# Three eighths of the last w2 block moved to 16 partitions on four DMA engines, and w_mod loaded in two pieces instead of three

## Chip, cores, metric

One core of one Trainium2 chip. The metric is the device time of one execution in microseconds (us). PE is the matrix engine, DVE, ACT and POOL are the vector, scalar and general engines, SP is the sync engine, which issues the loads. Every run also lists its **span**, the time from the first to the last instruction that the profiler recorded. Time minus span is called *outside*.

## The reference, cut to what matters

```python
mod = silu(c) @ w_mod                       # c: 2 x 1024, w_mod: 1024 x 6144
h = layernorm(x) * (1 + ca) + sa
x = x + ga * attention(h, k_cache, v_cache, wq, wo)   # 4 KV heads, 32768 positions, 32 query heads, batch 2
h = layernorm(x) * (1 + cb) + sb
y = gelu(layernorm(h) @ w1 + b1)            # 3584 wide
x = x + gb * (y @ w2 + b2)                  # w2: 3584 x 1024
```

Two tokens meet 178.28 MB of caches and weights, so this is a kernel that streams. `w_mod` opens the stream and `w2` closes it.

## The kernel before

The stream is issued from the sync engine (SP). The pieces that the change and the argument touch:

```python
WMOD_ITEMS = ((0, 1), (1, 4), (4, 8))       # rows of w_mod per load: lines of 12, 36, 48 KB a partition
W2_ITEMS = ((0, 8, 96), (8, 16, 112), (16, 24, 128), (24, 27, 144), (27, 28, 150))   # blocks of w2 per load
...
w2_v = B_w2.rearrange("(p j) n -> p j n", j=FT)      # 28 blocks of 128 rows x 1024 columns
for m, (j0, j1, off) in enumerate(W2_ITEMS):
    add(("w2", m), [j1 - j0, DM], w2_v[:, j0:j1, :], off * KB)
```

w2 comes in five loads: blocks 0 to 7, 8 to 15, 16 to 23, 24 to 26, and 27 alone. The tail multiplies the first 16 blocks with the activations as the stationary side, turns that result into columns with eight fp32 matmuls, and adds the last 12 blocks with the weights as the stationary side:

```python
for g in range(16):                          # blocks 0-15
    it = need("w2", m)
    for hf in range(2):
        pe(... matmul(psS[0][32*t:32*t+32, :], lhsT=gT[:, g, :], rhs=w[:, j, hf*512:(hf+1)*512] ...))
load_row("dve", psS[0], "psS0", 3)           # DVE copies the sums to SBUF
to_columns(psO, "psO", 3, True, False)       # eight fp32 matmuls (four calls in the code)
for g in range(16, FT):                      # blocks 16-27
    it = need("w2", m)
    for k in range(KT8):                     # eight matmuls a block
        pe(... matmul(psO[:, 2*k:2*k+2], lhsT=w[:, j, k*128:(k+1)*128], rhs=gT[:, g, 0:2] ...))
dve(mT = psO * mod(5)); dve(res_bf = mT + x1b); pe(transpose); dve(copy); store the output
```

## Time and profile before

| | before |
|---|---|
| time, median of 6 runs beside the changed kernel | 420.12 us (419.97 to 420.19) |
| span of the profiled run | 418.7 us |
| last semaphore increment of the load: blocks 8-15, 16-23, 24-26, 27 | 408.37, 413.23, 415.12, 415.76 us |
| last of the closing matmuls issued; output store issued | 416.02; 417.34 us |

Read the table from its end. The output is stored 1.3 us after the last matmul of w2, and that matmul comes 0.9 us after blocks 24 to 26 have landed. A load counts as landed when the last of its 16 increments has come, so the slowest of the 16 DMA engines decides. Two lines of the tail, from the timeline of the kernel before (start, duration, engine, line, operation, operands and shapes, count, and in brackets the idle time before it and what ended it):

```profile
408.41 1.90 PE L720 MATMUL psS<-w,gT 128*32 128x512 bf16 x16 [3.69 <-DMA w<-in_B_w_dram]
411.11 1.87 PE L668 MATMUL psZ<-half,S_sb 128*128 128x4 f32 x8 [0.80 <-DVE S_sb L664]
```

PE waits 3.69 us for blocks 8 to 15, multiplies them, and then waits for the DVE copy before it makes the columns. Those end just before blocks 16 to 23 land.

### The profile page before, as it was taken

Reading aid. Unit: us, or ns where it says so; the run is one execution under the profiler, and the core shown is the slowest. Engines: PE = TensorE matmul, PEld = TensorE weight load, DVE = VectorE, ACT = ScalarE, POOL = GpSimd, SP = SyncE. Lnnn points to the kernel's source line nnn. Section 1 sums busy time; section 2 is a strip of 40 time slices with the busy share of each in tenths; the row PEclk is TensorE's granted clock in tenths of the full one; section 3 lists DMA queues with packets and bytes.
Section 4 is the critical chain, followed back from the end, with each engine's and each line's share of the span. In section 5 each row is a group of like instructions: output and inputs, shape, how many; then the busy total and the mean of one; then the engine's idle time right before and its main releaser. Section 6 shows DMA issues by size and latency. Waiting matters only on the chain.

```text
span 418.7 us, 11609 instructions
## 1 busy us (share of the span) xinstructions
PE 291.0 (70%) x5183; PEld 231.3 (55%) x5183; DVE 209.6 (50%) x423; ACT 149.4 (36%) x179; POOL 6.8 (2%) x29
## 2 busy tenths in 40 slices
PE   1407449766996895699369957976995699564536
PEld 1104219762993794299149926962894399221214
DVE  1201105546677676467726664766477567620411
ACT  2000015533565364256405632643365166400100
POOL 3000000000000000000000000000000000000000
PEclk9999557986896997799589958986697889576585
DMA  9989999999999999999999999999999999899995
GB/s 373 450 380 449 448 404 493 398 406 446 441 432 429 423 451 429 419 454 457 391 435 476 407 416 448 438 438 426 438 438 426 416 460 457 377 448 428 424 427 249
DMA packets 5581, 178.42 MB, mean 426 GB/s; under 512 B 698, under 2 KB 706, under 8 KB 964
## 3 DMA queue, kind: packets, MB, share of 16 engines
q1 hardware_dynamic: 5572, 178.28, 98.8%
q8 instruction: 8, 0.13, 0.1%
q14 instruction: 1, 0.01, 0.0%
HBM read 178.28 MB, written 0.00 MB: 426 GB/s over the span
## 4 chain that ended last, share of the span: by engine, by line
DMA 71%; PE 24%; DVE 2%; issue 1%; ACT 1%; SPq 1%
DMA V<-in_A_v_cache_dram 39%; DMA wo<-in_A_wo_dram 10%; DMA K<-in_A_k_cache_dram 10%; PE psZ L584 10%; DMA w<-in_B_w_dram 9%; PE psKT L536 8%; DMA wmod<-in_w_mod_dram 4%; PE psS L548 1%; PE psZ L548 1%; PE psS L655 1%; PE psZ L729 1%; PE psZ L469 1%; ACT KT_sb L540 0%; PE psS L469 0%; DVE m1c L553 0%
## 5 line engine op out<-in xcount | busy, mean ns | idle before, releaser
L536 PE MATMUL psKT<-ident,K 128*128 128x128 bf16 x2048 | 163.1, 229 | 11.5 <-DMA K<-in_A_k_cache_dram 11.5
L540 ACT ACTIVATE KT_sb<-psKT 128x1024 bf16<-128x1024 bf16 x96 | 98.2, 1025 | 124.4 <-PE psKT L536 124.4
L542 DVE COPY KT_sb<-psKT 128x1024 bf16<-128x1024 bf16 x160 | 106.7, 688 | 61.6 <-PE psKT L536 61.2
L536 PEld LDWEIGHTS psKT<-ident,K 128*128 128x128 bf16 x2048 | 126.7, 102 | 13.0 <-DMA K<-in_A_k_cache_dram 12.7
L584 PE MATMUL psZ<-V,E_sb 128*32 128x512 bf16 x512 | 46.4, 541 | 23.2 <-DMA V<-in_A_v_cache_dram 20.0
L548 PE MATMUL psS<-qcur,KT_sb 128*128 128x8 bf16 x1024 | 44.7, 167 | 2.2 <-issue 2.2
L584 PEld LDWEIGHTS psZ<-V,E_sb 128*32 128x32 bf16 x512 | 18.7, 130 | 47.7 <-issue 38.8
L548 PE MATMUL psZ<-qcur,KT_sb 128*128 128x8 bf16 x1024 | 43.0, 167 | 2.2 <-issue 1.5
L548 PEld LDWEIGHTS psS<-qcur,KT_sb 128*128 128x128 bf16 x1024 | 40.0, 97 | 2.3 <-issue 2.3
L548 PEld LDWEIGHTS psZ<-qcur,KT_sb 128*128 128x128 bf16 x1024 | 37.9, 96 | 3.4 <-issue 1.6
L572 ACT ACTIVATE E_sb<-S_sb 128x512 bf16<-128x512 f32 x32 | 19.5, 630 | 29.6 <-DVE S_sb L570 29.6
L570 DVE TENSOR_TENSOR S_sb<-S_sb,gmb 128x512 f32<-128x512 f32 x32 | 20.0, 685 | 0.3
L576 DVE TENSOR_REDUCE rs<-E_sb 128x8 f32<-128x512 bf16 x32 | 19.7, 675 | 0.0
L469 PE MATMUL psS<-wmod,inT 128*32 128x512 bf16 x32 | 5.1, 624 | 16.2 <-DMA wmod<-in_w_mod_dram 16.2
L553 DVE TENSOR_REDUCE m1c<-psZ 128x8 f32<-128x512 f32 x16 | 11.1, 693 | 10.2 <-ACT S_sb L552 10.1
L595 DVE RECIPROCAL rinv<-psM 128x1 f32<-128x1 f32 x8 | 1.3, 168 | 27.7 <-PE psM L593 27.7
L605 PE MATMUL psM<-msum,hmat 128*128 128x128 f32 x16 | 4.2, 347 | 13.3 <-DVE msum L600 13.3
L559 PE MATMUL psM<-identf,m 128*8 128x128 f32 x16 | 4.3, 369 | 13.1 <-DVE m L556 13.1
L553 DVE TENSOR_REDUCE m1c<-psS 128x8 f32<-128x512 f32 x16 | 11.1, 693 | 3.2 <-ACT S_sb L552 3.1
L552 ACT ACTIVATE S_sb<-psZ 128x512 f32<-128x512 f32 x16 | 9.5, 595 | 7.5 <-PE psZ L548 7.5
L477 DVE COPY S_sb<-psS 128x512 f32<-128x512 f32 x1 | 0.7, 690 | 22.9 <-PE psS L469 22.9
L469 PEld LDWEIGHTS psS<-wmod,inT 128*32 128x32 bf16 x32 | 1.1, 132 | 19.3 <-DMA wmod<-in_w_mod_dram 18.0
(123 smaller groups left out, 167.5 us busy)
## 6 DMA issues: line engine op xcount, KB each, us to landing
K<-in_A_k_cache_dram SPq DMA_DIRECT2D x16, 4096.0 KB, 27.1
wq<-in_A_wq_dram SPq DMA_DIRECT2D x2, 4096.0 KB, 44.8
wo<-in_A_wo_dram SPq DMA_DIRECT2D x2, 4096.0 KB, 39.0
w<-in_B_w_dram SPq DMA_DIRECT2D x2, 3584.0 KB, 32.5
wmod<-in_w_mod_dram SPq DMA_DIRECT2D x1, 6144.0 KB, 29.8
w<-in_B_w_dram SPq DMA_DIRECT2D x3, 2048.0 KB, 37.8
wmod<-in_w_mod_dram SPq DMA_DIRECT2D x1, 4608.0 KB, 15.8
wmod<-in_w_mod_dram SPq DMA_DIRECT2D x1, 1536.0 KB, 6.0
```

The lines of the kernel that those rows point to most:

```text
L469: pe(lambda e, w=it.view, k=k, kk=kk, ch=ch, n=n, q=q: e.matmul(bank[n][32 * q:32 * q + 32, :], lhsT=inT[:, k, :], rhs=w[:, kk, ch * 512:( ...
L536: pe(lambda e, kq=kq, jj=jj, w=kt, t=t: e.transpose(psKT[kq][:, jj * 128:(jj + 1) * 128], w[:, t, :], ident[:, :]), reads=[it.reg, "ident" ...
L540: act(lambda e, src=src: e.activation(KT_sb[g8][:, :, :], src, ACT.Copy), reads=[f"psKT{kq}"], writes=[f"KT_sb{g8}"], sem=f"ev{cc}_{g8}")
L542: dve(lambda e, src=src: e.tensor_copy(KT_sb[g8][:, :, :], src), reads=[f"psKT{kq}"], writes=[f"KT_sb{g8}"], sem=f"ev{cc}_{g8}")
L548: pe(lambda e, t=t, jj=jj: e.matmul(ps[:, t * HPG:(t + 1) * HPG], lhsT=KT_sb[g8][:, jj, :], rhs=qcur[:, :], start=True, stop=True), reads= ...
L552: act(lambda e: e.activation(Sc, ps.rearrange("p (t h) -> p h t", h=HPG), ACT.Copy), reads=[preg], writes=[f"S_sb_{cc}"], sem=f"sc{cc}")
L553: dve(lambda e: e.tensor_reduce(m1c[:, :, cc], ps.rearrange("p (t h) -> p h t", h=HPG), AX.X, ALU.max), reads=[preg], writes=[f"m1c{cc}"])
L559: pe(lambda e: e.matmul(psM[0:HPG, 0:128], lhsT=m1[:, :], rhs=identf[:, :], start=True, stop=True), reads=["m1", "identf"], writes=["psM"])
L570: dve(lambda e: e.tensor_tensor(Sc, Sc, gmb[:, :].unsqueeze(2).to_broadcast([128, HPG, TPC]), ALU.subtract), reads=[f"S_sb_{cc}", "gmb"], ...
L572: act(lambda e: e.activation(Ec, Sc.rearrange("p h (u t) -> p u h t", t=4), ACT.Exp, scale=SCALE), reads=[f"S_sb_{cc}"], writes=[f"E_sb_{c ...
L576: dve(lambda e: e.tensor_reduce(rs4[:, :, cc], Ec.rearrange("p u h t -> p h u t"), AX.XY, ALU.add), reads=[f"E_sb_{cc}"], writes=[f"rs4_{c ...
L584: pe(lambda e, t4=t4, tg=tg, q=q: e.matmul(psO[32 * q:32 * q + 32, :], lhsT=E_sb[:, tg // 4, :, :].rearrange("p h t -> p (h t)"), rhs=vt[: ...
```

## The change

The intent: in this kernel some DMA engines are through earlier than others. The change takes three eighths of the last block (384 of 1024 columns) out of the closing load and gives them to engines 0 to 3, earlier in the stream. To make the sync engine put a load on four engines only, each piece is 16 partitions by 768 B, with a source whose outermost dimension is 4; eight such pieces hold the block's 128 rows. The activations for them have to be brought to 16 partitions as well (`selp`, `gx`). And w_mod comes in two loads instead of three.

```diff
-WMOD_ITEMS = ((0, 1), (1, 4), (4, 8))
+WMOD_ITEMS = ((0, 3), (3, 8))
+W2_CUT = 640
...
+    w2x = sb("w2x", [16, 8, DM - W2_CUT], BF16)
+    gx = sb("gx", [16, 8, 2], BF16)
+    selp = sb("selp", [128, 128], BF16)
...
-        add(("w2", m), [j1 - j0, DM], w2_v[:, j0:j1, :], off * KB)
+        n1 = W2_CUT if j1 == FT else DM
+        add(("w2", m), [j1 - j0, n1], w2_v[:, j0:j1, 0:n1], off * KB)
...
+    T.inst("pool", lambda e: e.tensor_copy(selp..., ident...), ...)      # a permuted identity
...
+    for q in range(8):                                                   # after the loads of wo are issued
+        src = w2_v[16 * q:16 * q + 16, FT - 1, W2_CUT:DM].rearrange("(b a) n -> a b n", a=4)
+        T.dma("sp", lambda e, q=q, src=src: e.dma_start(w2x[:, q, :], src), key=f"ld_w2x{q}", writes=[f"w2x{q}"])
...
+        if g == 8:                                                       # before blocks 8-15
+            for q in range(8):
+                pe(lambda e, q=q: e.matmul(psM[0:16, 56 + 2 * q:58 + 2 * q], lhsT=selp[:, 16 * q:16 * q + 16], rhs=gT[:, FT - 1, 0:2], start=True, stop=True), ...)
+            act(lambda e: e.activation(gx[:, :, :], psM[0:16, 56:72]..., ACT.Copy), reads=["psM"], writes=["gx"])
...
     to_columns(psO, "psO", 3, True, False)
+    for q in range(8):                                                   # 24 matmuls on 16 partitions
+        for k in range(W2_CUT // 128, KT8):
+            pe(lambda e, q=q, k=k: e.matmul(psO[:, 2 * k:2 * k + 2], lhsT=w2x[:, q, ...], rhs=gx[:, q, :], start=False, stop=False, ...), ...)
...
-        for k in range(KT8):
+        for k in range(KT8 if g < FT - 1 else W2_CUT // 128):            # block 27: five instead of eight
```

(Left out are the flags that close the accumulation.)

More of the change, by code (lines that the diff above doesn't have):

```diff
@@ L411, in bass_adaLN_cond__gqa_block_cached__mixer_channel_mlp__decode_kernel @@
     T.inst("pool", lambda e: e.memset(onesf[:, :], 1.0), writes=["onesf"])
+    T.inst("pool", lambda e: e.tensor_copy(selp.rearrange("p (q a b) -> p q a b", q=8, a=4), ident.rearrange("p (q b a) -> p q a b", q=8, a=4)),
+           reads=["ident"], writes=["selp"])
     for t, nm in [(inT, "inT"), (gT, "gT")] + [(atT[g], f"atT{g}") for g in range(G // 2)]:
@@ L715, in bass_adaLN_cond__gqa_block_cached__mixer_channel_mlp__decode_kernel @@
     for g in range(16):
+        if g == 8:
+            for q in range(8):
+                pe(lambda e, q=q: e.matmul(psM[0:16, 56 + 2 * q:58 + 2 * q], lhsT=selp[:, 16 * q:16 * q + 16], rhs=gT[:, FT - 1, 0:2], start=True, stop=True),
+                   reads=["selp", "gT"], writes=["psM"], mark=(q == 7))
+            act(lambda e: e.activation(gx[:, :, :], psM[0:16, 56:72].rearrange("p (q b) -> p q b", b=2), ACT.Copy), reads=["psM"], writes=["gx"])
         m, j = w2_of[g]
@@ L724, in bass_adaLN_cond__gqa_block_cached__mixer_channel_mlp__decode_kernel @@
     to_columns(psO, "psO", 3, True, False)
+    for q in range(8):
+        for k in range(W2_CUT // 128, KT8):
+            pe(lambda e, q=q, k=k: e.matmul(psO[:, 2 * k:2 * k + 2], lhsT=w2x[:, q, k * 128 - W2_CUT:(k + 1) * 128 - W2_CUT], rhs=gx[:, q, :],
+                                            start=False, stop=False, skip_group_check=True),
+               reads=[f"w2x{q}", "gx"], writes=["psO"], mark=False)
     for g in range(16, FT):
@@ L727, in bass_adaLN_cond__gqa_block_cached__mixer_channel_mlp__decode_kernel @@
         it = need("w2", m)
-        for k in range(KT8):
+        for k in range(KT8 if g < FT - 1 else W2_CUT // 128):
             pe(lambda e, w=it.view, g=g, j=j, k=k: e.matmul(psO[:, 2 * k:2 * k + 2], lhsT=w[:, j, k * 128:(k + 1) * 128], rhs=gT[:, g, 0:2],
-                                                            start=False, stop=(g == FT - 1), skip_group_check=True),
-               reads=[it.reg, "gT"], writes=["psO"], mark=(k == KT8 - 1 and g in (23, 26, 27)))
+                                                            start=False, stop=(g == FT - 1 or (g == FT - 2 and k >= W2_CUT // 128)), skip_group_check=True),
+               reads=[it.reg, "gT"], writes=["psO"], mark=((k == KT8 - 1 and g in (23, 26)) or (g == FT - 1 and k == W2_CUT // 128 - 1)))
     dve(lambda e: e.tensor_tensor(mT[:, :, :], psO[:, 0:16].rearrange("p (k b) -> p k b", b=2), mod(5), ALU.mult), reads=["psO", "modT"], writes=["mT"])
```

## The prediction

> **What bounds the kernel now.** I read the page first: its slices, its chain and its queues.
>
> ```profile
> DMA  9989999999999999999999999999999999899995
> ...
> DMA 71%; PE 24%; DVE 2%; issue 1%; ACT 1%; SPq 1%
> ...
> q1 hardware_dynamic: 5572, 178.28, 98.8%
> q8 instruction: 8, 0.13, 0.1%
> q14 instruction: 1, 0.01, 0.0%
> HBM read 178.28 MB, written 0.00 MB: 426 GB/s over the span
> ```
>
> The 16 DMA engines are full in every slice but the last. The kernel is a stream of 178.28 MB at 426 GB/s, and only three things can move its end: the bytes and packet costs of the engine that finishes last, the start before the first packet, and the tail after the last load. Note the instruction queues: eight packets of 16 KB and one of 8 KB also ran on these engines.
>
> Then the pieces of the chain in order of time, for the tail:
>
> ```profile
> 375.40 37.83 DMA w<-in_B_w_dram
> 413.27 1.87 PE psZ L729 x64
> 415.17 1.03 PE psZ L729 x32
> ```
>
> The last wait on a load in this chain is that for blocks 16 to 23 of w2 (PE starts at 413.27). Then 64 small matmuls run, then 24 for blocks 24 to 26 and 8 for block 27. The instruction records show how tight this is. The matmuls follow each other every 26.7 ns at a granted clock of 0.5. The first 64 were issued by 414.98; blocks 24 to 26 had their last semaphore increment at 415.12 and PE went on at 415.17; block 27 landed at 415.76, and its first matmul started at 415.81, with no gap after the 24. So block 27's landing is hidden, by 0.05 us; **the landing of blocks 24 to 26 sets the end**, 24 + 8 matmuls ahead of the closing additions:
>
> ```profile
> 413.27 2.91 PE L729 MATMUL psZ<-gT,w 128*128 128x2 bf16 x96 [0.30 <-DMA w<-in_B_w_dram]
> 416.22 0.17 DVE L732 TENSOR_TENSOR mT<-psZ,modT 128x16 f32<-128x16 f32 x1 [5.17 <-PE psZ L729]
> 416.43 0.23 DVE L733 TENSOR_TENSOR res_bf<-mT,x1b 128x16 bf16<-128x16 f32 x1
> ```
>
> Last, the trace's DMA packet records and the increments of each load's semaphore, which no view prints. Each engine works back to back, so its packets can be strung together by end and start. The 16 engines are not level. Block 27's last packets end at 413.8 to 414.2 on seven engines, at 414.70 on one, and at 415.16 to 415.44 on eight; an increment follows about 0.33 us after. Every one of the eight late ones lost about 1.3 us at one 16 KB instruction packet; the middle one lost some 0.6 us at the 8 KB one, at 84.8 us.
>
> **What the Trainium skill says.** First, "DMA: Bandwidth & Descriptors", section "Why a DMA increments its semaphore by 16 and not by 1": a load issued from the sync engine is split over the largest k up to 16 that divides the slowest dimensions of both sides, and takes the lowest-numbered k engines. The trace agrees: the b2 pieces of 1, 2, 4 and 1 rows gave 256 B packets on four engines, nested: four on one, two on one, one each on two. For a piece of the change (source outermost 4, destination 16 partitions) k is 4: engines 0 to 3. Secondly, the same page, "Where 436 GB/s comes from": 435 GB/s at most; here a 64 KB packet takes 2414 ns from start to start, 27.1 GB/s an engine, 434 for sixteen. So nothing is left in the rate. Thirdly, the same page, "Why small descriptors are slow (HBM only)": a fixed overhead per packet. Start to start this trace has 14 ns for 256 B, 37 for 896 B, 80 for 2 KB, 230 for 6 KB, 456 for 12 KB, 1360 for 36 KB, 1811 for 48 KB and 2414 for 64 KB: about 36.8 ns a KB and some 4 ns a packet; a semaphore packet is 6 ns. Fourthly, "TensorE: Matmul & The Clock Gate", section "Weight-path perf modes — Fast Weight Load (FWL) and DoubleRow": fast weight load is on with 128 weights that are not fp32. The 26.7 ns of line 729 agree; that it holds for weights on only 16 partitions, no line shows cleanly.
>
> **The change, part by part.**
>
> *w_mod in two loads.* Each engine now carries 8 packets of 12, 36 and 48 KB: 3648 + 10880 + 14488 = 29016 ns. Then 8 of 36 and 8 of 60 KB; 60 KB lies between 48 and 64 at 2263 ns: 10880 + 18104 = 28984. With one semaphore packet less that is 0.04 us off every engine. It also makes c and x land behind 36 KB lines instead of 12: some 8 x (1360 - 456) = 7.2 us later, 14 us instead of 7. Then three rows of w_mod are multiplied where one was, and five after the second landing at 31.8 instead of four, 1.28 us more. That pushes wq's first half from 44.9 to about 46.2 and its end from 48.4 to 49.7; the second half waits for its landing at 52.75 in any case, so this is absorbed. The queue is full to 60 us and more, so the K and V issues (the first V from 48.55 to about 49.8) starve nothing.
>
> *Block 27 cut to 640 columns.* 8 packets per engine of 1280 B (51.5 ns by the rule) for 2 KB (80): -0.23 us on every engine, in the last load only. Its matmuls go from 8 to 5: -0.08 us on the path.
>
> *Eight pieces on engines 0 to 3.* Each piece gives each of the four 4 packets of 768 B (32.7 ns) and a semaphore packet: 137 ns; eight make **1.09 us more on each of these four**, queued ahead of w1, so every load from there on is later on them. Their issues (8 x 0.33 us) fall in SP's wait between 345 and 355 and cost nothing.
>
> *PE.* Eight matmuls and an ACT copy for gx stand before block 8, where PE waits for 3.7 us: free. The 24 for the pieces follow the fp32 column matmuls, whose last issue is done at about 412.77: 24 x 26.7 = 0.64 us, to 413.41, so 0.14 past today's 413.27. The 64 then end at 415.12, just before blocks 24 to 26 could start at 415.13. Nearly free as well.
>
> *The sum.* The question is whether engines 0 to 3 have 1.09 us to spare. Following the b2 packets, three of the four are among the early ones (last data at 413.84, 413.93 and 414.19): with +1.09 - 0.27 they end at 414.66 to 415.01, below the late eight, which drop to 415.17. But the fourth is the middle one, 414.70, and goes to 415.52. In the loads before, its data for blocks 16 to 23 ended at 412.20 and for 24 to 26 at 414.06, against 412.93 and 414.78 of the latest engine. With +1.09 - 0.04 these become 413.25 and 415.11, so blocks 24 to 26 land at about 415.45 and PE takes them at 415.50 in place of 415.17. (Blocks 16 to 23 start at about 413.6, their 64 end at 415.3 to 415.45, in time.) Then 24 + 5 matmuls: 415.50 + 0.77 = 416.27; today 415.17 + 0.85 = 416.02. The sum is **+0.25 us**: 420.14 becomes about 420.4.
>
> **The rivals.** *A: the intended gain.* If the 8 KB instruction fetch falls on another engine in the new kernel, or comes with the profiler alone, all four have room. Then only 0.04 (w_mod) and 0.08 (three matmuls) are won, not the 0.23, as block 27's landing was hidden already: 420.0. For it: the b2 loads and this change both seem made on the view that these engines are early. Against: an 8 KB instruction packet on one of the four stands in the trace.
>
> *B: PE becomes the bound.* If weights on 16 partitions load slower, or eight waits for eight semaphores each cost PE something, the 24 matmuls take 1.5 to 3 us instead of 0.64; the spare time ends at 413.27, so the end moves by 0.9 to 2 us: 421 to 422. For it: the c transposes (two partitions, a strided source) came every 61 ns. Against: that source is strided, the new one is not, and a wait already satisfied (block 27's) cost no gap.
>
> *C: the start.* Packets of 36 KB at the start could ramp otherwise than those of 12 KB, which lost 0.5 to 0.7 us per engine in the first two; a few tenths either way: 419.8 to 420.6.
>
> *D: a moved clock.* The whole tail runs at 0.5. If the throttle pattern shifts, PE's part shrinks and some 0.4 us come off: 419.7.
>
> **Range and chances.** I give the sum +0.25 some 55%, rival A 30%, and the rest to B, C and D. The centre is 420.3, drawn a little from 420.4 towards A; 8 in 10 within 419.8 to 420.75. The 2% limits lie 8.4 us away; nothing above reaches them but an unforeseen stall in the stream, so within 2% has 0.985, slower 0.01, faster 0.005.
>
> **What would show it.** Right: packets of 768 B at 33 ns on four engines only, 1.1 us of added delay there; blocks 24 to 26 landing at about 415.4 with a middle engine last; the 24 new matmuls at 26.7 ns, in the pause before block 16; w_mod's last landing at 31.8 as before; wq's second half starting at 52.8. Wrong: a last landing of blocks 24 to 26 at 415.1 (then A), the 24 matmuls taking over 1 us (B), the first w_mod load off by more than 0.1 us from 8 x 1360 ns plus today's ramp (C), or another granted clock after 405 us (D). A change of over 1 us would mean that an engine did something which I have not seen here.

## The result and the profile after

| | before | after |
|---|---|---|
| time, median | 420.12 us (6 runs) | 420.69 us (6 runs, 420.50 to 421.06) |
| span, median | 418.8 us | 419.2 us |
| outside, each run | 1.25 to 1.37 us | 1.46, 1.96, 1.76, 1.42, 1.40, 1.40 us |
| blocks 8-15, 16-23, 24-26, 27 landed | 408.37, 413.23, 415.12, 415.76 | 408.80, 413.62, 415.46, 415.87 |
| last closing matmul issued; store issued | 416.02; 417.34 | 416.54; 417.85 |

(Span and outside of before are from the 38 runs of it that ran beside the experiments; the landings and issues are those of the profiled run.) The ratio is 1.0016, with a 95% interval of 1.0003 to 1.0028. A ratio here is the mean time of one kernel's fast runs over that of the other's of the same rounds, so it isn't quite the ratio of the medians quoted. The change is a loss of 0.57 us in the median: some 0.4 in the span and the rest outside it.

The page of the profile after, the lines that answer to those of before:

```profile
DMA  8989999999999999999999999999999999999995
...
DMA 77%; PE 20%; DVE 1%; issue 1%; ACT 1%; SPq 0%
...
q1 hardware_dynamic: 5588, 178.28, 98.6%
q8 instruction: 9, 0.15, 0.1%
...
HBM read 178.28 MB, written 0.00 MB: 425 GB/s over the span
```

The stream is the same: the same bytes, the engines full in nearly every slice. One line differs in kind: queue 8 now carries nine instruction packets instead of eight.

The chain that ended last, in order of time (start, duration, engine, what):

```profile
369.77 39.04 DMA w<-in_B_w_dram
408.85 1.93 PE psS L736 x12
410.80 0.70 DVE S_sb L675
411.54 1.87 PE psZ L679 x8
413.41 0.73 PE psZ L743 x24
414.13 2.58 PE psZ L750 x93
```

Compare this with the chain of before. There, the last DMA wait was that for blocks 16 to 23, and the matmuls fell into 64 and 32 with a landing between. Here the last DMA wait is one load earlier, that for **blocks 8 to 15**. From 408.85 on everything is compute, one thing on the heels of the next, and the loads of blocks 16 to 27 don't appear any more. The timeline says the same:

```profile
408.85 1.90 PE L736 MATMUL psS<-w,gT 128*32 128x512 bf16 x16 [3.24 <-DMA w<-in_B_w_dram]
...
411.54 1.87 PE L679 MATMUL psZ<-half,S_sb 128*128 128x4 f32 x8 [0.79 <-DVE S_sb L675]
...
413.34 0.79 PE L743 MATMUL psZ<-gx,w2x 16*128 16x2 bf16 x24
...
414.06 2.64 PE L750 MATMUL psZ<-gT,w 128*128 128x2 bf16 x93
416.74 0.17 DVE L753 TENSOR_TENSOR mT<-psZ,modT 128x16 f32<-128x16 f32 x1 [5.26 <-PE psZ L750]
```

Lines 743 and 750 carry no bracket, so PE didn't idle before them. Against before, line 736 (which was 720) starts 0.44 us later, and the closing group (93 matmuls, 96 before) starts 0.79 later and ends 0.52 later. The closing additions on DVE start 0.52 later, too.

Last, the packets, strung together engine by engine (an ordinary table, worked out from the trace's DMA records; times are those at which an engine's data of a load ended; where there is a dash, a record is missing):

```
                                    8-15     16-23    24-26    27
late one of engines 0-3, before     407.35   412.21   414.06   414.70
  the same, after                     -      413.28   415.13   415.55
latest other of 0-3, before         406.84   411.70   413.55   414.20
  the same, after                   407.74   412.61   414.44   414.88
latest of engines 4-15, before      408.07   412.94   414.79   415.43
  the same, after                   408.44   413.30   415.14   415.56
```

The late one of the four is exactly where the prediction put it: 413.28, 415.13 and 415.55 against 413.25, 415.11 and 415.52. The packets cost what was said as well: 128 of 768 B at 32 to 33 ns from start to start, on four engines alone. In this one trace a second engine, which had started late and then met an instruction packet, ended at the same time. The landing doesn't hang on that chance: in w2_only below, without it, blocks 24 to 26 landed at 415.51.

### The profile page after: what moved, and what is told of

The parts are those of the page before. It is cut to its first block, busy times and chain, and to the rows that moved or that the text cites. A ratio compares the mean times of both kernels' runs of the same rounds, so it can differ in the third digit from the quotient of the medians.

```text
span 419.3 us, 11677 instructions
## 1 busy us (share of the span) xinstructions
PE 294.7 (70%) x5212; PEld 236.3 (56%) x5212; DVE 209.7 (50%) x423; ACT 149.6 (36%) x180; POOL 7.0 (2%) x30
## 4 chain that ended last, share of the span: by engine, by line
DMA 77%; PE 20%; DVE 1%; issue 1%; ACT 1%; SPq 0%
DMA V<-in_A_v_cache_dram 54%; PE psZ L591 11%; DMA K<-in_A_k_cache_dram 10%; DMA w<-in_B_w_dram 9%; PE psKT L543 4%; DMA KT_sb<-in_c_dram 3%; PE psS L555 1%; PE psZ L555 1%; PE psZ L476 1%; PE psZ L750 1%; PE psS L736 0%; PE psZ L679 0%; PE psS L476 0%; ACT KT_sb L547 0%; SPq L394 0%
## 5 line engine op out<-in xcount | busy, mean ns | idle before, releaser
L543 PE MATMUL psKT<-ident,K 128*128 128x128 bf16 x2048 | 165.8, 231 | 14.1 <-DMA K<-in_A_k_cache_dram 14.1
L543 PEld LDWEIGHTS psKT<-ident,K 128*128 128x128 bf16 x2048 | 129.4, 104 | 15.6 <-DMA K<-in_A_k_cache_dram 15.6
L662 PE MATMUL psS<-wo,atT 128*32 128x512 bf16 x64 | 6.8, 603 | 7.1 <-DMA wo<-in_A_wo_dram 7.1
```

The source lines that it names most:

```text
L543: pe(lambda e, kq=kq, jj=jj, w=kt, t=t: e.transpose(psKT[kq][:, jj * 128:(jj + 1) * 128], w[:, t, :], ident[:, :]), reads=[it.reg, "ident" ...
L662: pe(lambda e, w=it.view, m=m, j=j, hf=hf, q=q: e.matmul(psS[0][32 * q:32 * q + 32, :], lhsT=atT[m][:, j, :], rhs=w[:, j, hf * 512:(hf + 1 ...
```

## The experiments

Two theories stood at the start. The first is that of the prediction with a correction: the four engines' 1.09 us makes the late one last, **and** the 24 matmuls, coming after a later landing of blocks 8 to 15, keep PE from ever waiting again. The rival was w_mod (the engine that started late in the trace after would speak for it). After the first four runs (wmod_only to w2_896) a third came up, that nothing in the data stream matters, but the length of the program: a ninth instruction packet, and the time outside. The twelve kernels of the first three groups tell these apart; the last three follow up what the twelve had left open. Each group ran on one chip with its own runs of the kernel before: 420.10, 420.14, 420.12 and 420.11 us in the median. All the results were right.

| label | median us | ratio (95%) | span, median | outside |
|---|---|---|---|---|
| wmod_only | 420.13 | 1.0003 (0.9989 to 1.0017) | 418.8 | 1.29 to 1.33 |
| w2_only | 420.75 | 1.0016 (1.0002 to 1.0029) | 419.3 | 1.35 to 1.45 |
| w2_early | 420.71 | 1.0015 (1.0002 to 1.0029) | 419.1 | 1.35, 1.42, 2.00, 1.81, 1.83 |
| w2_896 | 420.70 | 1.0014 (1.0000 to 1.0027) | 418.9 | 1.68 to 2.38 |
| pad33 | 420.12 | 1.0000 (0.9987 to 1.0014) | 418.8 | 1.25 to 1.34 |
| one_384 | 421.52 | 1.0027 (1.0013 to 1.0040) | 419.8 | 1.37 to 1.93 |
| one_256 | 420.79 | 1.0015 (1.0001 to 1.0028) | 419.1 | 1.38 to 1.94 |
| best | 420.51 | 1.0011 (0.9998 to 1.0025) | 419.1 | 1.33 to 1.89 |
| pad_act | 420.26 | 1.0003 (0.9989 to 1.0017) | 418.8 | 1.32 to 1.36, once 1.77 |
| pad_pool | 420.03 | 0.9997 (0.9984 to 1.0011) | 418.7 | 1.31 to 1.33 |
| pad_loads16 | 420.18 | 1.0000 (0.9986 to 1.0014) | 418.9 | 1.27 to 1.38 |
| pad_loads768 | 420.45 | 1.0005 (0.9991 to 1.0018) | 419.1 | 1.30 to 1.36 |
| w2_896_dve | 421.52 | 1.0021 (1.0008 to 1.0034) | 419.5 | 1.28 to 1.42, once 2.77 |
| after_dve | 420.60 | 1.0011 (0.9998 to 1.0024) | 419.3 | 1.27 to 1.34 |
| best2 | 420.14 | 1.0004 (0.9992 to 1.0017) | 418.8 | 1.28 to 1.36, once 2.27 |

What is argued from here on are tenths of a microsecond, so spans (listed to 0.1) and landings carry more than the ratios do.

### wmod_only: the kernel before with the two w_mod loads alone

```diff
-WMOD_ITEMS = ((0, 1), (1, 4), (4, 8))
+WMOD_ITEMS = ((0, 3), (3, 8))
```

> The kernel before with only w_mod's split changed to two loads of 36 and 60 KB lines. Theory (two causes): the trace of the changed kernel has one engine whose first packet starts 0.8 us after the others and that then stays late, 14.04 us at the end of the first w_mod load against 13.3 to 13.7; with an instruction packet on top it is one of the two engines that finish last. If the 36 KB lines at the start do that, this kernel alone is 0.3 to 0.45 us slower than before, its last increment for w2's blocks 8 to 15 at 408.7 to 408.8 instead of 408.37. Rival (the pieces alone are to blame, the late engine was one execution's chance): within 0.05 us of before, or 0.04 faster as predicted.

Measured: 420.13 against 420.10 us, spans as before. The w_mod part neither gains nor costs. It does what it looks like: the little loads behind it come later. The line that transposes `c` waits for it, first in the timeline of before, then in that of the changed kernel:

```profile
7.07 0.63 PE L416 MATMUL psM<-ident,KT_sb 2*128 2x2 bf16 x8 [7.07 <-DMA KT_sb<-in_c_dram]
```

```profile
14.20 0.62 PE L423 MATMUL psM<-ident,KT_sb 2*128 2x2 bf16 x8 [14.20 <-DMA KT_sb<-in_c_dram]
```

The 7 us are gone again before they reach the tail: the second half of wq landed at 52.81 us in the changed kernel, and PE is waiting for it in both. The late start of one engine, seen in the trace after, is not something that this part brings in every run.

### w2_only: the changed kernel with the three w_mod loads of before

```diff
-WMOD_ITEMS = ((0, 3), (3, 8))
+WMOD_ITEMS = ((0, 1), (1, 4), (4, 8))
```

> The changed kernel with w_mod in its three old loads. Theory (two causes, which overlap rather than add, since a load lands with its slowest engine): the engine of the four that lost time at the 8 KB instruction packet ends blocks 16 to 23 at about 413.28 against 412.93 for the slowest before, blocks 8 to 15 land at about 408.75, and the whole is still 0.4 to 0.6 us slower than before. Rival (the start is to blame alone): blocks 8 to 15 land at 408.4, and what remains is PE's detour of 24 matmuls, 0 to 0.2 us.

Measured: 420.75 us, and a span of 419.3 (419.3 to 419.5), half a microsecond over that of before. So the whole loss is in the w2 part. In its trace the late one of the four ended at 413.34 (blocks 16 to 23) and 415.19 (24 to 26), later than the second latest engine (413.00 and 414.85). Blocks 8 to 15 had landed at 408.84, and PE worked without a wait from there: 24 new matmuls from 413.38, the others from 414.11, the last issued at 416.58.

### w2_early: w2_only with the 24 matmuls before the column matmuls

There PE waits for the DVE copy anyhow.

```diff
     load_row("dve", psS[0], "psS0", 3)
-    to_columns(psO, "psO", 3, True, False)
     for q in range(8):
         for k in range(W2_CUT // 128, KT8):
-            pe(... start=False, stop=False ...)
+            pe(... start=(q == 0 and k == W2_CUT // 128), stop=False ...)
+    to_columns(psO, "psO", 3, False, False)
```

> As w2_only, but the 24 matmuls of the pieces stand before the column matmuls, in the 0.75 us in which PE waits for DVE's copy of the first half. Theory: in the changed kernel PE has no wait from the landing of blocks 8 to 15 on, because the 24 matmuls and the gap before them cost 0.85 us where only 0.5 us was spare; freed of them PE waits for blocks 24 to 26 again, which land at about 415.45: 0.15 to 0.3 us faster than w2_only, so 0.2 to 0.35 slower than before. Rival (the late landings alone set the end, wherever the matmuls stand): the same as w2_only within 0.05 us.

From its timeline:

```profile
410.98 0.79 PE L742 MATMUL psZ<-gx,w2x 16*128 16x2 bf16 x24
...
411.84 1.87 PE L679 MATMUL psZ<-half,S_sb 128*128 128x4 f32 x8
...
413.97 2.76 PE L750 MATMUL psZ<-gT,w 128*128 128x2 bf16 x93 [0.26 <-DMA w<-in_B_w_dram]
```

The bracket is back: PE waits for blocks 16 to 23 again. In the instruction records it waits for blocks 24 to 26 as well: the 64th of these matmuls is issued at 415.67, the next at 415.79, with the landing at 415.75. The landings themselves were later in this trace (409.10 for blocks 8 to 15). The spans came down to 418.9 to 419.3, in the median 419.1 for 419.3: about 0.2 us. The time doesn't show it, since three of the five runs had 1.8 to 2.0 us outside. This was not foreseen.

### w2_896: one eighth of the block instead of three

```diff
-W2_CUT = 640
+W2_CUT = 896
```

(against w2_only; 128 columns in pieces of 256 B, 8 matmuls in place of 24)

> As w2_only, but only the last 128 columns of block 27 are moved: pieces of 256 B lines. Theory: each piece is 4 x 14 + 6 ns, eight are 0.5 us instead of 1.09; the late one of the four engines ends blocks 8 to 15 at 407.85, under the 408.07 of the slowest, so no load lands later than before, PE does 8 matmuls more and one fewer at the end, and the time is before's within 0.08 us (0.03 faster by the sum). Rival (it is the eight loads with their semaphores, the added instructions or the extra waits, not the bytes): nearly as slow as w2_only, 0.3 us or more over before.

The span fell to 418.7 to 419.1 (418.9 in the median), within 0.1 of before, as the theory of the late engine and of PE says. The pieces cost 0.6 to 0.7 us on each of the four, where 0.5 had been expected. But the time stayed at 420.70, with 1.68 to 2.38 us outside the span in all five runs. In the profiled run a 16 KB instruction packet ran at 420.12 and an 8 KB one at 420.46, both after the span's end at 418.9. So there is a second cost, and it isn't in the span.

### pad33: the kernel before, with 33 unused matmuls in the pause before blocks 8 to 15

```diff
     for g in range(16):
+        if g == 8:
+            for q in range(33):
+                pe(... matmul(psM[0:16, ...], lhsT=ident[:, 0:16], rhs=gT[:, FT - 1, 0:2] ...))
```

> The kernel before with 33 matmuls added in PE's wait ahead of block 8, their results unused, nothing else changed: PE's program is about as much longer as in w2_only. New theory (program length): w2_896 was as slow as w2_only although its span was only 0.1 us longer; what grew is the time outside the span, 1.3 us in every run of before against 1.7 to 2.4 there, and its trace has a ninth 16 KB instruction packet at 420.12, after the end of the work, which the kernel before hasn't. So the longer program of PE alone costs: span as before within 0.1 (418.7 to 419.0), a ninth 16 KB instruction packet after 415 us, time 420.4 to 421.0. Rival (the loads and their semaphores make the time outside the span longer): 420.1, no ninth packet, 1.3 us outside the span.

Measured: 420.12 against 420.14 us, the outside 1.25 to 1.34. The page of its profile:

```profile
q8 instruction: 9, 0.15, 0.1%
```

Only PE instructions were added, and queue 8 went from eight packets to nine, so queue 8 is where PE's program is fetched. The ninth packet came at 416.23 us and cost nothing. A longer PE program by itself is not the cause.

### one_384 and one_256: one load onto 128 partitions, on four engines, instead of eight

```diff
-    for q in range(8):
-        src = w2_v[16 * q:16 * q + 16, FT - 1, W2_CUT:DM].rearrange("(b a) n -> a b n", a=4)
-        T.dma("sp", lambda e, q=q, src=src: e.dma_start(w2x[:, q, :], src), ...)
+    src_x = w2_v[:, FT - 1, W2_CUT:DM].rearrange("(b a) n -> a b n", a=4)
+    T.dma("sp", lambda e: e.dma_start(w2x[:, :], src_x), key="ld_w2x", writes=["w2x"])
```

(384 columns, and 256 with `W2_CUT = 768`; 3 and 2 matmuls in place of 24, one for the activations in place of eight)

> As w2_only (384 columns on the same four engines, w_mod in three loads), but as one load onto 128 partitions in permuted order: 1 matmul and a copy make the permuted gT, 3 matmuls take the place of 24, and one semaphore that of eight. The bytes per engine are the same, 32 x 33 + 6 = 1.05 us. Theory (late engine + program length): the late one of the four still ends blocks 24 to 26 at about 415.15 and the span is 0.25 to 0.35 longer than before, 419.0 to 419.2; no ninth instruction packet, 1.3 us outside the span; time 420.3 to 420.45. Rival (PE's detour and program alone): the time is before's within 0.05.

> As one_384 with 256 columns moved: 32 packets of 512 B, 0.75 to 0.8 us on each of the four engines. Theory: the late one of the four ends blocks 8 to 15 at 408.1 to 408.15, level with the slowest of before (408.07 to 408.2), so the span is before's within 0.07 and the time 420.05 to 420.2. If the late engine isn't the cause of the 0.3 us of one_384, this one is as slow as that.

Both missed. one_384 was the slowest of the second group, 420.77 to 424.96 us, spans 419.4 to 423.1. In the profiled run, that of 424.96, all 16 engines ran slower from this load to the end: the first increments of w1's two loads are 9.49 us apart, against 8.47 in w2_only. In the traces of one_256 and of best (below), with the same kind of load, the packets of all 16 engines get longer at the same place, but for one packet each: 1.11 to 1.34 us for 28 KB in place of 1.06. In the traces with eight pieces at most five engines have such a packet. So the single load and the disturbance go together in three traces of three; why it reaches twelve engines that don't carry the load, and why it lasted in one_384, is not known. one_256 had spans of 418.9 to 419.2 and up to 1.94 us outside; with few matmuls added it still has a late engine, so it tells little about PE. The disturbance is a reason to leave the eight pieces as they are in the later experiments.

### best: one_256 with blocks 24-25, 26 and 27 as three loads

```diff
-W2_ITEMS = (..., (24, 27, 144), (27, 28, 150))
+W2_ITEMS = (..., (24, 26, 144), (26, 27, 148), (27, 28, 150))
```

> A try at a version that beats both: one_256 with blocks 24 and 25, 26 and 27 as three loads instead of 24 to 26 and 27. Blocks 24 and 25 land 0.6 us earlier, block 26 as 24 to 26 did, block 27 at 415.64 instead of 415.76, and after it PE has 6 matmuls left instead of 24 + 8 after 415.17: the sum is 415.69 + 0.16 = 415.85 against 416.02 before, 0.1 to 0.2 us faster than before: 419.9 to 420.0. Rival: the packets and semaphore added and the late engine eat it: 420.1.

Measured: 420.51 us (420.13 to 420.81), no better than the kernel before and above what the rival gave, too.

### pad_act, pad_pool, pad_loads16, pad_loads768: one added cost each, on the kernel before

```diff
# pad_act
+            act(lambda e: e.activation(gx[:, :, :], gT[0:16, 0:8, 0:2], ACT.Copy), reads=["gT"], writes=["gx"])
# pad_pool
+    T.inst("pool", lambda e: e.tensor_copy(selp..., ident...), reads=["ident"], writes=["selp"])
# pad_loads16: the eight loads with lines of 16 B, and PE waits for them before blocks 8-15
+        src = w2_v[16 * q:16 * q + 16, FT - 1, 1016:DM].rearrange("(b a) n -> a b n", a=4)
# pad_loads768: the same with lines of 768 B; block 27 stays whole, and no matmul is added
+        src = w2_v[16 * q:16 * q + 16, FT - 1, 640:DM].rearrange("(b a) n -> a b n", a=4)
```

> The kernel before with one small ACT copy added ahead of block 8, as the change adds one; its result is unused. What is open: with the moved columns the time outside the span is 1.35 to 2.0 us instead of 1.26 to 1.35, and every profiled run with over 1.7 has an 8 KB instruction packet after the span's end, which before and pad33 (a longer PE program) haven't. If ACT's program is the one that outgrew what had been fetched: some runs with 1.7 us or more outside the span, span as before (418.7 to 419.0). If it isn't ACT's: 1.26 to 1.35 outside in all runs, time 420.1.

> The kernel before with the one POOL copy (selp) that the change adds; unused. If POOL's program is the one that outgrew what had been fetched: some runs with 1.7 us or more outside the span, span as before. If not: 1.26 to 1.35 outside, time 420.1.

> The kernel before with the eight loads of the change onto 16 partitions added, each line cut to 16 bytes, unused (PE waits for them long after they have landed). If the program of the sync engine (which issues loads) is the one: some runs with 1.7 us or more outside the span. If it isn't: 1.26 to 1.35. In either case the four engines get 4 x 8 tiny packets, some 0.2 us, which the late one of them has to spare: span 418.7 to 418.95.

> The same with the lines of 768 B of the change; block 27 stays whole and PE does no added matmul. Theory (the late one of the four engines): 1.09 us more there, its data for blocks 24 to 26 end at about 415.15 and the span is 0.3 to 0.45 us longer than before with PE waiting for that load: 419.1 to 419.3; with PE's detour (w2_only, 419.3 to 419.5) it was 0.5 to 0.65. Rival (the detour is all): span as before, 418.8.

pad_loads768 is the one that isolates the engines. Its spans are 419.0 to 419.2, in the median **+0.3 us** over 418.8, with the outside as before. The late one of the four ended at 413.46 and 415.31, the latest of all 16; blocks 24 to 26 landed at 415.63. From its timeline:

```profile
409.05 1.90 PE L727 MATMUL psS<-w,gT 128*32 128x512 bf16 x16 [3.80 <-DMA w<-in_B_w_dram]
...
413.82 2.87 PE L736 MATMUL psZ<-gT,w 128*128 128x2 bf16 x96 [0.21 <-DMA w<-in_B_w_dram]
```

Here PE still waits (the bracket before line 736), because nothing stands between the columns and block 16. So this is the cost of the late engine without the 24 matmuls. pad_loads16 gives the same engines eight loads of next to no bytes. They cost some 0.6 us on each of the four, where 0.2 had been expected, and the time did not move (420.18): with 0.6 us the late one stays below the eight latest. The packet records say where the rest went: the 32 short packets and their semaphore packets took 0.23 us, as expected, but the first 28 KB packet behind them took 1.40 to 1.46 us on these engines in place of 1.06. (In w2_896 it took 1.19 to 1.28; behind lines of 768 B it took the usual 1.06.) That agrees with the prediction's own numbers, by which the late one had 414.78 - 414.06 = 0.72 us to spare.

pad_pool costs nothing. pad_act cost nothing in the span, and in one of five runs the outside was 1.77 us.

### w2_896_dve and after_dve: the one added ACT instruction put on DVE

```diff
-            act(lambda e: e.activation(gx[:, :, :], psM[0:16, 56:72]..., ACT.Copy), ...)
+            dve(lambda e: e.tensor_copy(gx[:, :, :], psM[0:16, 56:72]...), ...)
```

> The changed kernel with the copy of gx on DVE instead of ACT. Theory: no run has over 1.5 us outside the span; the span keeps the late engine and PE's detour, 419.2 to 419.5; time 420.5 to 420.8, about 0.1 less than the changed kernel's 420.69 in the mean, and without its runs of 421.06. Rival: runs of 421 still occur, with 1.7 us or more outside.

> w2_896 (five runs of five with 1.7 to 2.4 us outside the span) with the copy of gx on DVE instead of ACT: ACT's program is then as long as before. Theory (ACT's longer program makes an 8 KB instruction load fall after the work): 1.26 to 1.45 us outside the span in every run, no 8 KB packet after the end, span 418.7 to 419.0, time 420.05 to 420.25. Rival (anything else of the change): still 1.7 or more in most runs, 420.6 to 420.8.

after_dve is the changed kernel with that edit alone. The outside is 1.27 to 1.34 us in all five runs, that of the kernel before, where the changed kernel had 1.40 to 1.96. The spans stay at 419.1 to 419.4. This fits the ACT instruction as the cause of the time outside: the copy is the only instruction that the change adds on ACT.

w2_896_dve was expected to be the best of all, and two of its six runs (420.08 and 420.22) are as fast as before. The other four are at 421.46 to 421.81: three have spans of 420.1 to 420.5, and one has a span of 418.8 and 2.77 us outside. The profiled run is one of the three. It has the same work up to the issue of the output's store (417.44 us), and then SP waits for the store's end. The waits of SP, this kernel's first, then that of before:

```profile
SPq L765 <- DMA out_dram<-c: 2.3, 1, 2.3
```

```profile
SPq L744 <- DMA out_dram<-c: 0.6, 1, 0.6
```

Waiting for the 4 KB of output took 2.3 us in place of 0.6. PE's ninth instruction packet came at 418.24 in this run, while the output was being stored. Of the store's 16 increments 15 had come by 418.80, and the last came at 420.48, so a single engine was held: 3.04 us after the store's issue, against 1.36 in w2_896 (418.84 from 417.48). The packets show what held it: fifteen of the store's 256 B packets started between 418.29 and 418.43, the sixteenth at 419.43, as the instruction packet ended (419.45). The span is 420.5 for that wait alone. In the traces in which the ninth packet came at 416.23 (pad33), 416.62 (after_dve), 416.72 (w2_early) or 417.19 us (after), before the store, it cost nothing that the span shows.

The Trainium skill has a section on this, "Runtime: NRT & Kernel Launch", "Instruction fetch mechanics": an engine's program is refilled in blocks of 16 KiB, ahead of execution, by a DMA queue that its sequencer drives, and crossing a block boundary is called "mostly hidden". The traces agree with the size (nine packets of 16 KB). They don't agree with hidden, in two ways. First, PE does stop: in each of the 17 traces it stands still at least once between 75 and 88 us, between two matmuls of the same group, with 1.5 to 4.3 us from one matmul's start to the next's, and goes on 1.3 to 1.6 us after a 16 KB packet has ended. That these stops are waits for instructions is inferred from this agreement in time. In the trace of before two of the packets end at 76.07 and 83.55 us, and its timeline has

```profile
77.35 0.22 PE L548 MATMUL psZ<-qcur,KT_sb 128*128 128x8 bf16 x3 [1.49 <-issue]
84.88 0.25 PE L548 MATMUL psS<-qcur,KT_sb 128*128 128x8 bf16 x4 [2.24 <-issue]
```

("issue" is idle time for which the profile shows no other cause.) No span shows these stops: before has two of them, pad_act one, at spans of 418.7 and 418.8. Secondly, each packet sets back the DMA engine that carries it, and that does cost in a kernel which the DMA engines bound.

### best2: one eighth of the block, gx on DVE, its 8 matmuls early, and three last loads

```diff
 W2_CUT = 896
-W2_ITEMS = (..., (24, 27, 144), (27, 28, 150))
+W2_ITEMS = (..., (24, 26, 144), (26, 27, 148), (27, 28, 150))
...
+    # the 8 matmuls stand before to_columns, as in w2_early; gx is copied on DVE
```

> A second try at a version that beats both: only 128 columns moved (the late one of the four has room for them), gx copied on DVE, the 8 added matmuls in PE's wait for DVE's copy, and blocks 24 and 25, 26, 27 as three loads. PE then is bound by blocks 16 to 23 (413.27) and 64 + 24 + 7 matmuls, 415.8, or by block 27's landing at about 415.74 and 7 matmuls, 415.93, against 416.02 before: 0.1 us faster than before, 420.0 to 420.05, if nothing else shows; the spread of before, 0.1, may hide it. Rival: 420.1 to 420.2, as the loads' extra packets and semaphores cost what is won.

Measured: 420.14 against 420.11 us; spans of 418.7 to 418.8, one run of five with 2.27 us outside although ACT has no added instruction. So DVE in place of ACT is not a cure in every case, and nothing tried here beats the kernel before.

## Why the prediction was right or wrong

**Right: the late engine.** The step "415.50 in place of 415.17" rests on one engine of the four that has no 1.09 us to spare. The engine's ends came out within 0.03 us of the text, the landing of blocks 24 to 26 at 415.46 against 415.45. pad_loads768 shows its cost alone, +0.3 us, and pad_loads16 that 0.6 us on the same engines is free. The direction and the range (419.8 to 420.75 against 420.69) held.

**Wrong: "in time", and "nearly free".** The failed step is the one on PE: the 24 matmuls end at 413.41, blocks 16 to 23 start at about 413.6, "their 64 end at 415.3 to 415.45, in time". Block 16 started at 414.06, and the first matmul of blocks 24 to 26 at 415.79, 0.33 us after they had landed. The trace tells which terms were short:

| term of PE's way to block 16 | predicted | after |
|---|---|---|
| delay of blocks 8 to 15, passed on to the columns | 0 | +0.43 |
| last column matmul issued to first new one | about 0.15 | 0.29 |
| the 24 matmuls, first to last, and on to the next | 0.64 | 0.63 + 0.09 |

The first term is the large one, and it is an inconsistency, not a surprise. The prediction said that every load from w1 on is later on the four engines, and then used it for the loads of blocks 16 to 26 alone; for the columns it kept today's 412.77. Blocks 8 to 15 are carried by the same engines and landed later too. So the pause into which the 24 were to fall had moved away. Alone that would have cost little: by an estimate from the prediction's own numbers (412.77 + 0.43 + 0.64, and 64 matmuls of 26.7 ns) PE then comes to blocks 24 to 26 at 415.55, where they can start at 415.50. The two small terms, 0.14 and 0.09, go on top of it and make 415.78. With the predicted landing and no queue on PE, the end would have come at 415.50 + 0.77 = 416.27, the +0.25 of the text. It came at 416.54: the missing 0.27 is PE's queue in this pair of traces. In spans over several runs it is about 0.2 (w2_only 419.3, w2_early 419.1), as a single trace of before can have its landings 0.1 to 0.2 earlier than another: blocks 8 to 15 landed at 408.37 in that of before, and at 408.45 to 408.57 in those of pad_act, pad_loads16, wmod_only and pad33, whose spans don't differ.

**Missing: the time outside the span.** The sum had no term for it. It went from 1.31 us in the mean of the runs of before to 1.57 in the mean of the six after, +0.26; in the median it is some +0.1. after_dve puts it back to where it was by moving one instruction off ACT. What happens there is argued and not shown: the profiled runs of w2_896, one_384 and one_256, all with over 1.7 us outside, have an 8 KB instruction packet after the last work, as if an engine fetched one more block of its program before the execution counts as done. pad_act, with that instruction alone, shows it in one run of five; w2_only, which has the instruction as well, hardly at all; and best2 shows it once without it. So where in the program the block boundary falls must play a part, and that stays open.

**Right, for little: w_mod.** 0.04 us less was predicted and nothing was to be seen (wmod_only, +0.03 in the median; the interval of the ratio reaches from 0.5 us less to 0.7 more). That the later start of `c` would be absorbed by the wait for wq held.

**The packets and the matmuls.** 33 ns for 768 B, 1.09 us per engine, 2263 ns for 60 KB (2267 measured) and 26.7 ns for matmuls with weights on 16 partitions all held, and so did the gain of 0.23 us in the last load that is hidden behind blocks 24 to 26.

**Small misreadings, without effect on the sum.** Strung packet by packet in the trace of before, a 16 KB instruction packet sets its engine back by 1.42 us and the 8 KB one by 0.84 (0.87 to 0.95 and 0.31 until the next packet starts, and some 0.5 by which that packet is longer). The 1.3 and 0.6 of the text are about what the groups of engines are apart at the end; the sum used the ends themselves. The eight issues took 5.41 us (345.45 to 350.86), not 8 x 0.33, still within SP's wait. And w_mod landed at 32.21 before and 32.51 after; 31.8 was its first increment.

**The rivals.** A, the intended gain, did not come, since the late engine of the four is there in every trace that was taken apart. B was right that PE becomes the bound, but for another reason than the one given: the 24 took 0.63 us and not 1.5. C (the start) fell with wmod_only. D did not show: the tail's matmuls kept their 26.7 ns.

So the sum that the runs support is: late engine +0.3, PE's queue +0.2 and the three matmuls saved −0.08, which makes +0.4 in the span; then +0.1 outside in the median, and up to 0.6 in a single run.

## What to carry to other kernels

When work is put on some of the DMA engines, list every load behind it, with the slowest engine of each, and carry the delay through the whole tail: a pause of another engine, into which new work is to go, may move or close with it. An average says that four engines have room; the landing is set by the one that has least. And add a line for the program itself: instruction blocks are fetched over the same DMA engines, and one that falls on the output's store can cost more than the change wins. Whether one after the last work does, too, is open.

## What the Trainium skill lacked or had wrong

- "Runtime: NRT & Kernel Launch", "Instruction fetch mechanics": it calls the crossing of a block boundary mostly hidden. In these traces a 16 KB instruction packet sets its DMA engine back by 1.42 us and an 8 KB one by 0.84, where a 16 KB packet of data takes 0.61. Eight such packets are why eight engines end late here, and one that met the output's store in w2_896_dve made the wait for it 2.3 us instead of 0.6. PE itself stops for 1.5 us and more beside some of these packets in every trace.
- No page tells of a time outside the span that differs between kernels with nearly the same work: 1.25 to 1.37 us in 38 runs of before, up to 2.77 with a handful of instructions added (w2_896_dve). The length of PE's program alone doesn't do it (pad33, 1.25 to 1.34).
- "DMA: Bandwidth & Descriptors", "Why small descriptors are slow (HBM only)": a fixed overhead per packet doesn't give the cost of tiny loads in a full stream, as the first large packet behind them is longer, too. Eight loads of four 16 B packets per engine cost 0.6 us on each of the four, eight of 256 B 0.6 to 0.7, eight of 768 B 1.09.
- No page has it that a load on four engines can go together with slower packets on the other twelve: in the profiled run of one_384 the first increments of w1's loads are 9.49 us apart, 8.47 in w2_only.
